# A planner that counts TensorE's instruction chunks, and 64-wide products with the running sums

## The chip, the cores and the metric

The kernel runs on one core of a Trainium2 chip. A core has TensorE for matrix products (PE in the profile, with its weight loads as PEld), VectorE (DVE), ScalarE (ACT), GpSimd (POOL), and SyncE (SP), which here issues nearly all DMA transfers. Products are written to PSUM, a memory of eight banks; everything else lies in SBUF or in HBM. The metric is the device time of one execution in microseconds. Lower is better. Three runs of the kernel before took 935.92, 937.82 and 938.09 us.

## The reference

Two blocks follow each other. The first is a retention layer over 8 batches, 8 heads, 576 positions and head size 64: a causal product of queries and keys, weighted by a power of a per-head decay, applied to the values. Its output becomes 4608 tokens of 512 numbers. The second is a two-layer network with a leaky activation whose slope below zero is one number per hidden unit.

```
scores = scale * np.matmul(q, k.transpose(0, 1, 3, 2))
gamma = 1.0 - 2.0 ** (-5.0 - np.arange(H))
Dmat = np.where(rel >= 0, gamma[:, None, None] ** rel[None, :, :], 0.0)
x = np.matmul(scores * Dmat, v)          # then (B,H,S,D) -> (B*S, H*D)
h = x @ w_in                             # 512 -> 2048
g = np.maximum(h, 0.0) + alpha * np.minimum(h, 0.0)
out = g @ w_out                          # 2048 -> 512
```

All inputs and outputs are 32-bit floats.

## The kernel before

The positions of a batch are cut into nine chunks of 64. Within a chunk the retention is computed directly; what earlier chunks contribute comes through running sums of key times value, one 64 by 64 matrix per head.

The first two batches are handled in "parts": part 0, 1 and 2 are batch 0 (chunks 0 to 3, 4 to 7, and 8), parts 3, 4 and 5 are batch 1. Parts 0, 1, 3 and 4 are the large ones. A large part goes through `part_transposes` (L448: q and k are turned on TensorE), `part_scores` (L472, then a mask on DVE at L478), `part_states` (L494, summed up on DVE at L506 and L508), and `part_values`. The last one has two steps into the same two PSUM banks `pv`: first the products within a chunk (L541), then, in L557, the products of the queries with the running sums, added on top. L557 issues each product in two halves of 32 output rows, so 32 products for two chunks. Then ScalarE copies the result to the token block x (L572). Parts 2 and 5 are handled by `last_part` (L593, L606, L619, L626).

The other six batches go through `joint`, one pair of heads at a time, 24 pairs: values of the pair before (L809), then scores and states of this pair (L860, L867, L870), in array shapes of 128x64 and 64x64. Their sums travel by DMA from `su` into `vn` before the next L809 may use them.

The network works on blocks of 256 tokens. The first eight units use plain 32-bit products (L1039 in, L1070 out), while the weights are still being converted (ScalarE L670 and L672, DVE L680, L682, L691, GpSimd L694). Later units (L1108 in, L1189 out, and L1138 for two blocks at once) use numbers split into pieces, one pass each. Units and attention work are interleaved on TensorE.

How they are interleaved is decided by a planner that runs when the program is built. Every step is recorded with `do(engine, cost, function, reads, writes)`; `plan()` first walks backwards and gives every step a due time, then walks forwards engine by engine: of the steps that could start within `SLACK` of the earliest, it takes the one due first. `SWITCH` adds 0.1 us where PE's step is of another `kind` than the one before. The instructions are then written out in the planned order, on each engine, so that order is fixed; the costs decide the order, not the real time. DMA transfers are steps too, on SP; in the first 100 planned us, an SP transfer also waits so that at most 1.25 MB (`IN_FLIGHT`) are under way.

A 32-bit product is two passes on PE, each of a weight load and a matmul instruction, so four instructions; a transpose or a product of pieces is one pass, two instructions.

Of the kernel before, what the change touches and what calls it, by code (L numbers as in the profile page):

```python
# [21 lines left out]
def kernel(  # L22
# [72 lines left out]
    a16 = const.tile([NFC, P], FP32, name="a16")  # L95
    malpha = const.tile([P, NFC], FP32, name="malpha")

    gam = [1.0 - 2.0 ** (-5.0 - h) for h in range(H)]
# [54 lines left out]
    class Op:  # L153
        def __init__(self, eng, cost, fn, deps, banks, late, lock, hold):
            self.eng, self.cost, self.fn, self.deps = eng, cost, fn, deps
            self.banks, self.late, self.lock, self.hold = banks, late, lock, hold
            self.n = len(ops)

# [17 lines left out]

    def do(eng, cost, fn, r=(), w=(), late=0.0, lock=False, kind=None, hold=0.0):
# [10 lines left out]
        op = Op(eng, cost, fn, None, [g.slot for g in gens if g.slot and g.slot.bank], late, lock, hold)  # L188
# [35 lines left out]
    def plan():  # L224
# [42 lines left out]
        free, held, port, wire, kinds = dict(BEGIN), {}, [0.0, ""], 0.0, {e: e for e in BEGIN}  # L267
        can = [0.0] * len(ops)
        for op in ops:
            if not op.deps:  # L270
                ready[op.eng].append(op)

        def earliest(op):
            t = max(free[op.eng], can[op.n], op.hold)
            for b in op.banks:
                if b in held:
                    t = max(t, max([x + LAT.get(e, 0.1) for e, x in held[b].items()
                                    if e != op.eng] or [0.0]))
            if op.lock and port[1] != op.eng:
                t = max(t, port[0])  # L280
            if op.late:
                t = max(t, wire - BACKLOG, due[op.n] + last - HOLD)
            return t + SWITCH.get(op.eng, 0.0) * (kinds[op.eng] != op.kind)

        while len(order) < len(ops):
            pick = None
            for e, queue in ready.items():
                if not queue:
                    continue
                c = [(earliest(op), op) for op in queue  # L290
                     if e != "PE" or op.n <= rest[0] + AHEAD_PE]
                if not c:
                    continue
                t0 = min(t for t, _ in c)
                t, op = min((x for x in c if x[0] <= t0 + SLACK.get(e, 0.05)),
                            key=lambda x: (due[x[1].n], x[1].n))
                if pick is None or t < pick[0]:
                    pick = t, op
            t, op = pick
            ready[op.eng].remove(op)  # L300
            if op.eng == "PE":
                rest.remove(op.n)
            begin[op.n] = t
            kinds[op.eng] = op.kind
            free[op.eng] = end[op.n] = t + op.cost
            if op.late:
                wire = max(wire, t + op.cost) + op.late
                end[op.n] = wire
            for b in op.banks:
                held.setdefault(b, {})[op.eng] = t + op.cost  # L310
            if op.lock:
                if port[1] == op.eng or t + op.cost > port[0]:
                    port[:] = [t + op.cost, op.eng]
            order.append(op)
            for u in users[op.n]:
                left[u.n] -= 1
                can[u.n] = max(can[u.n], end[op.n] + wait(op, u))
                if not left[u.n]:
                    ready[u.eng].append(u)
        total = max(end)  # L320
        return total, order, begin, end

    AHEAD_PE = 150
    BACKLOG, HOLD = 2.0, 30.0
    LAG, HOLD_X = 2, 100.0
    PUMP0, PUMP = ((1, 1), (0, 1), (0, 1), (0, 1)), ((1, 2), (1, 2), (0, 1), (0, 1))
    GROUPS = (("v0",), ("v1",), ("x", "su"))
    SLACK, SWITCH = {"PE": 0.3}, {"PE": 0.1}
    BEGIN = {"PE": 3.8, "ACT": 0.5, "DVE": 5.5, "POOL": 5.4, "SP": 0.5}
# [61 lines left out]
    def key_p(x, i, m):  # L391
        return (room[x, i], "d", m) if x % 3 < 2 else (room[x, 0], "d", i)
# [43 lines left out]
    def part_transposes(x, i, bank):  # L436
# [6 lines left out]
        for m in range(2):  # L443
            pt = Gen(next(bank))

            def f(m=m, pt=pt):
                for c in range(NPAIR):
                    nc.tensor.transpose(pt.get()[:, c * P:(c + 1) * P],  # L448
                                        part(x, i)[:, m, 2 * c:2 * c + 2].rearrange(
                                            "p h d -> p (h d)"), ident)  # L450
            do("PE", 0.6 if x else 1.0, f, [key_p(x, i, m)], [(pt, 0)])

# [5 lines left out]
    def part_scores(x, bank):  # L458
# [7 lines left out]
        for m in range(2):  # L466
            def f(m=m):
                for c in range(NPAIR):
                    for p2 in range(2):
                        for h2 in range(2):  # L470
                            j = chunk(2 * m + p2)
                            nc.tensor.matmul(  # L472
                                ps[h2].get()[half(p2), (2 * c + m) * C:(2 * c + m + 1) * C],
                                kT()[half(h2), c, j], qT()[half(h2), c, j], start=True, stop=True)
            do("PE", 0.6, f, [(kt, "t", m), (qt, "t", m)], [(ps[0], m), (ps[1], m)])
        for h2 in range(2):
# [7 lines left out]
    def part_states(x, bank):  # L484
# [4 lines left out]
        for m in range(2):  # L489
            def f(m=m):  # L490
                for c in range(NPAIR):
                    for p2 in range(2):
                        for h2 in range(2):
# [5 lines left out]
                                             skip_group_check=True)  # L499
            do("PE", 0.6, f, [key_p(x, 0, m), key_p(x, 2, m)], [(pu[0], 0), (pu[1], 0)])  # L500
        for j in range(4):
# [25 lines left out]
    def part_values(x, bank):  # L527
# [7 lines left out]
        for m in range(2):  # L535
            def f(m=m):
                for c in range(NPAIR):
                    for p2 in range(2):
                        for h2 in range(2):
# [5 lines left out]
                                             skip_group_check=True)  # L545
            do("PE", 0.6, f, [key_p(x, 2, m), (a, "m", 0), (a, "m", 1)], [(pv[0], 0), (pv[1], 0)])
# [32 lines left out]
    def last_part(x):  # L579
# [9 lines left out]
        def f():  # L589
            to = pt.get().rearrange("p (i c s) -> p i c s", i=2, c=NPAIR)  # L590
            for i in range(2):
                for c in range(NPAIR):
                    nc.tensor.transpose(to[:, i, c], part(x, i)[0:C, 0, 2 * c:2 * c + 2].rearrange(  # L593
                        "p h d -> p (h d)"), ident[0:C, 0:C])
        do("PE", 0.8, f, [key_p(x, 0, 0), key_p(x, 1, 0)], [(pt, 0)])
        do("ACT", 0.59, lambda: nc.scalar.copy(
# [11 lines left out]
        do("PE", 0.5, f, [(t, "t")], [(ps[0], 0), (ps[1], 0)])  # L608
        for h2 in range(2):
# [5 lines left out]
        def f():  # L615
# [6 lines left out]
            for c in range(NPAIR):  # L622
                for h2 in range(2):
                    for e in range(0, D, 32):
# [3 lines left out]
                                         skip_group_check=True)  # L628
        do("PE", 0.9, f, [key_p(x, 2, 0), (t, "m", 0), (t, "m", 1), (t, "t"), carry_key(x)], [(pv, 0)])
        gx, o = chunk_home(x, NJ - 1)  # L630
# [203 lines left out]
    def on_pe(parts, groups):  # L834
        for some in groups:
            do("PE", sum(parts[x][0] for x in some), lambda some=some: [parts[x][1]() for x in some],
               [key for x in some for key in parts[x][2]],
               [key for x in some for key in parts[x][3]])

# [187 lines left out]
    def unit_plain(cell):  # L1027
# [5 lines left out]
        for cc in range(2):  # L1033
            def mm(cc=cc):
                w = plain[4 * u + cc]
                for f in range(2):
                    for c2 in range(2):
# [18 lines left out]
    def second_plain(cell):  # L1056
# [9 lines left out]
        for m in range(2):  # L1066
            def mm(m=m, a=acc):
                for f in range(2):
# [4 lines left out]
                                     stop=(cell["last"] and f == 1))  # L1073
            do("PE", 1.75, mm, [(ga, 0), (ga, 1), plain[4 * u + 2], plain[4 * u + 3]],
               [(acc[m], 0)])
            if cell["last"]:
# [12 lines left out]
    def unit(cell):  # L1089
# [7 lines left out]
        for f in range(2):  # L1097
# [5 lines left out]
            def mm(f=f, at=at):  # L1103
# [7 lines left out]
            do("PE", 1.43, mm, x_keys(vis, side) +  # L1111
               [w_at[u, i][l] for i in range(2) for l in range(3)], [(ph, 0), (ph, 1)], kind="pieces")
            fc = 2 * u + f
# [14 lines left out]
    def unit_two(va, vb, u, ga, f):  # L1128
# [3 lines left out]
        def mm():  # L1132
# [7 lines left out]
        do("PE", 2.73, mm, x_keys(va, 0) + x_keys(vb, 1) +  # L1140
           [w_at[u, i][l] for i in range(2) for l in range(3)], [(p0, 0), (p1, 0)], kind="pieces")
        fc = 2 * u + f
# [31 lines left out]
    def second(cell):  # L1174
# [7 lines left out]
        for m in range(2):  # L1182

            terms = ((0, 0), (0, 1)), ((1, 2),)
            for some in reversed(terms) if cell["last"] else (sum(terms, ()),):
                def mm(m=m, a=list(acc), some=some):
# [8 lines left out]
                   [w_at[u, i][l] for i in (2, 3) for _, l in some],  # L1195
                   [(acc[2 * m + b], 0) for b in sorted({b for b, _ in some})], kind="pieces")
            if cell["last"]:
# [331 lines left out]
```

## Time and profile before

| what | value |
|---|---|
| median of three runs | 937.82 us |
| profiled execution, own time | 939.56 us |
| profiled span | 937.9 us |
| PE busy | 915.6 us, 98% of the span |
| POOL, ACT, DVE busy | 578.8, 552.8, 531.9 us |
| PE busy from 0 to 20 us, and from 20 to 40 | 11.67 and 14.54 us |
| PE busy from 40 to 105, 105 to 450, 450 to 938 | 63.11, 342.52, 483.75 us |
| DMA share in the same five stretches | 0.99, 1.00, 0.73, 0.77, 0.25 |
| L557 on PE | 448 passes |

The page lists each engine's busy time, then the span in forty slices with one digit each for the busy tenths, and then the DMA queues. PE's busy share says only that some product was under way. "Idle before" and the list of waits tell what ended each idle stretch of an engine: a semaphore set by another engine or a transfer, or "issue", when nothing that the profile shows was waited for. The chain is the path of work that ended last, in order of time; each row of it has a start, a length and what ran.

### The profile page before, as it was taken

The numbers are of one execution on the slowest core, as the hardware profiler recorded it, in microseconds if no ns is written. First come the engines' busy times: TensorE is split into PE (matmuls) and PEld (weight loads), VectorE is DVE, ScalarE is ACT, GpSimd is POOL, SyncE is SP. The second block draws the span as 40 slices with busy tenths as digits, with TensorE's granted clock in tenths as the row PEclk, the third lists the DMA queues.
The fourth block names the chain that finished last, engine by engine and source line by source line (L and its number), as shares of the span: only waits on it lengthen the run. The fifth ranks groups of instructions, "written<-read, shape, count | busy, mean of one in ns | idle before, by whom it ended". The sixth has DMA issues, their size and how long they took to land.

```text
span 937.9 us, 21264 instructions
## 1 busy us (share of the span) xinstructions
PE 915.6 (98%) x8241; PEld 778.5 (83%) x8241; DVE 531.9 (57%) x1070; ACT 552.8 (59%) x1175; POOL 578.8 (62%) x491
## 2 busy tenths in 40 slices
PE   6799999999999999999999999999999999999998
PEld 5576688988898898889899988888888888888887
DVE  6668566666776666766654764443444444444333
ACT  4366556566766665666775885645546463635342
POOL 5657766739676685664666465748374656647363
PEclk9999999999999999999999999999999999999999
DMA  9987487798888869965335421121212122221112
GB/s 233 226 200 137 131 197 159 157 205 188 196 189 197 204 152 196 196 148 151 113 113 191 125 90 68 46 90 45 90 45 91 58 89 88 78 71 45 45 45 68
DMA packets 235524, 120.94 MB, mean 129 GB/s; under 512 B 203408, under 2 KB 203424, under 8 KB 235424
## 3 DMA queue, kind: packets, MB, share of 16 engines
q1 hardware_dynamic: 235424, 119.59, 50.3%
q8 instruction: 65, 1.06, 0.5%
q14 instruction: 35, 0.29, 0.1%
HBM read 74.19 MB, written 31.98 MB: 113 GB/s over the span
## 4 chain that ended last, share of the span: by engine, by line
PE 92%; SPq 2%; DMA 2%; issue 1%; DVE 1%; POOL 1%; ACT 1%; POOLq 0%; ACTq 0%; DVEq 0%
PE pso L1189 38%; PE psh L1108 21%; PE psh L1138 9%; PE psa L1138 9%; PE psh L1039 3%; PE pso L1070 3%; PE psh L809 3%; SPq L206 2%; PE psa L870 2%; DMA op<-in_moe_w_out_dram 1%; DMA kn<-in_k_dram 1%; PE psh L860 1%; PE psa L867 1%; DMA w<-in_q_dram 1%; PE psa L472 0%
## 5 line engine op out<-in xcount | busy, mean ns | idle before, releaser
L1189 PE MATMUL pso<-w,g 128*128 128x512 f32 x1416 | 344.7, 391 | 0.0
L1189 PEld LDWEIGHTS pso<-w,g 128*128 128x128 f32 x1416 | 260.2, 188 | 50.6
L1108 PE MATMUL psh<-lx,w 128*128 128x256 f32 x1608 | 208.7, 285 | 0.0
L1108 PEld LDWEIGHTS psh<-lx,w 128*128 128x128 f32 x1608 | 202.0, 191 | 7.2 <-issue 0.5
L1168 POOL TENSOR_TENSOR g<-g 128x512 fp32r<-128x512 f32 x136 | 176.1, 1295 | 23.0 <-DVE w L1014 4.4
L1165 POOL TENSOR_TENSOR g<-ga,g 128x512 fp32r<-128x512 f32 x72 | 93.0, 1292 | 110.1 <-ACT g L1161 90.1
L1116 DVE SCALAR_TENSOR_TENSOR ga<-psh,ga 128x256 f32<-128x256 f32 x144 | 60.6, 421 | 67.5 <-ACT ga L1115 66.1
L1115 ACT COPY ga<-psh 128x256 f32<-128x256 f32 x144 | 53.6, 373 | 70.7 <-PE psh L1108 61.5
L1165 POOL TENSOR_TENSOR g<-x,g 128x512 fp32r<-128x512 f32 x40 | 51.7, 1294 | 63.8 <-ACT g L1161 61.3
L1122 DVE SCALAR_TENSOR_TENSOR ga<-psh,malpha,ga 128x256 f32<-128x256 f32 x144 | 68.9, 478 | 24.2 <-ACT psh L1119 23.4
L1018 POOL TENSOR_TENSOR lx<-lx 128x512 fp32r<-128x512 f32 x48 | 61.9, 1294 | 27.3 <-DVE lx L1014 12.7
L1119 ACT ACTIVATE psh<-ga 128x256 f32<-128x256 f32 x144 | 56.0, 389 | 28.0 <-DVE ga L1116 27.8
L1161 ACT ACTIVATE g<-ga 128x512 fp32r<-128x512 f32 x72 | 45.5, 632 | 25.0 <-DVE ga L1122 16.9
L1165 POOL TENSOR_TENSOR g<-vn,g 128x512 fp32r<-128x512 f32 x24 | 31.1, 1296 | 42.1 <-ACT g L1161 38.9
L888 DVE SCALAR_TENSOR_TENSOR at<-psa,pf,mask 64x512 f32<-64x512 f32 x48 | 36.0, 750 | 34.8 <-PE psa L867 33.9
L1163 ACT ACTIVATE g<-ga 128x512 fp32r<-128x512 f32 x72 | 45.0, 625 | 0.0
L1207 DVE TENSOR_TENSOR op<-pso,op 128x512 f32<-128x512 f32 x34 | 23.4, 687 | 36.5 <-PE pso L1189 36.4
L1161 ACT ACTIVATE g<-x 128x512 fp32r<-128x512 f32 x40 | 25.2, 632 | 32.0 <-PE pso L1189 16.1
L1145 DVE SCALAR_TENSOR_TENSOR x<-psh,x 128x512 f32<-128x512 f32 x20 | 13.8, 690 | 44.5 <-PE psh L1138 40.9
L809 PEld LDWEIGHTS psh<-at,vn 128*64 128x64 f32 x864 | 28.2, 137 | 12.6 <-issue 5.3
L1014 POOL TENSOR_TENSOR lx<-x,lx 128x512 fp32r<-128x512 f32 x24 | 31.0, 1294 | 12.2 <-DVE wa L682 6.2
L809 PE MATMUL psh<-at,vn 128*64 128x64 f32 x864 | 32.7, 226 | 2.5 <-DMA vn<-su 1.3
(289 smaller groups left out, 1695.5 us busy)
## 6 DMA issues: line engine op xcount, KB each, us to landing
xk<-x SPq DMA_DIRECT2D x18, 512.0 KB, 4.0
out_dram<-o SPq DMA_DIRECT2D x36, 256.0 KB, 4.2
ok<-o SPq DMA_DIRECT2D x34, 256.0 KB, 2.8
x<-xk SPq DMA_DIRECT2D x17, 512.0 KB, 5.0
op<-ok SPq DMA_DIRECT2D x17, 512.0 KB, 3.9
qx<-in_q_dram SPq DMA_DIRECT2D x96, 72.0 KB, 3.1
kx<-in_k_dram SPq DMA_DIRECT2D x96, 72.0 KB, 3.0
kn<-in_k_dram SPq DMA_DIRECT2D x48, 144.0 KB, 3.8
```

The source lines that it names most:

```text
L809: nc.tensor.matmul(pv[i].get()[half(h2), (j - js[0]) * C:(j - js[0] + 1) * C], vns[n % 2][:, h2, j], mt.get()[:, h2, j], start=True, stop= ...
L1018: lambda l=l, d=d, h=view(0, c): nc.gpsimd.tensor_tensor(out=piece(d()), in0=h(), in1=l(), op=ALU.subtract),
L1108: nc.tensor.matmul(at(b), w[:, c0:c0 + P], xp(l, cc), start=(n == 0 and cc == 0), stop=(n > 0 and cc == NCC - 1), skip_group_check=True)
L1115: do("ACT", 0.36, lambda g=g, at=at: nc.scalar.copy(g(), at(1)), [(ph, 1)], [(ga, f)])
L1116: do("DVE", 0.42, lambda g=g, at=at: nc.vector.scalar_tensor_tensor(out=g(), in0=at(0), scalar=ONE, in1=g(), op0=ALU.mult, op1=ALU.subtrac ...
L1119: do("ACT", 0.39, lambda g=g, at=at: nc.scalar.activation(at(1), g(), ACTF.Relu, scale=-1.0), [(ga, f)], [(ph, 1)])
L1122: do("DVE", 0.48, lambda g=g, at=at, fc=fc: nc.vector.scalar_tensor_tensor(out=g(), in0=at(1), scalar=malpha[:, fc:fc + 1], in1=g(), op0=A ...
L1138: nc.tensor.matmul(p.get(), w[:, c0:c0 + P], piece(words_of(g)[:, o:o + DM]), start=(l != 1 and cc == 0), stop=(l > 0 and cc == NCC - 1))
L1161: do("ACT", 0.64, lambda: nc.scalar.mul(piece(to.get()[:, 2]), whole(), BELOW), both, [(to, 2)])
L1165: do("POOL", 1.29, lambda: nc.gpsimd.tensor_tensor(out=piece(to.get()[:, 1]), in0=whole(), in1=to.get()[:, 2], op=ALU.subtract), both + [( ...
L1168: do("POOL", 1.29, lambda: nc.gpsimd.tensor_tensor(out=piece(to.get()[:, 2]), in0=to.get()[:, 0], in1=to.get()[:, 1], op=ALU.subtract), [( ...
L1189: nc.tensor.matmul(a[2 * m + b].get(), piece(g.get()[:, l, f, m * P:(m + 1) * P]), w_piece(u, 2 + f, l), start=(cell["first"] and f == 0 a ...
```

## The change

The planner learns how many PE instructions each step issues (`size`). It keeps a position in a chunk of `CHUNK` = 256 instructions, which starts 190 before the end of one; when a step carries the position over a chunk's end, it notes when the chunk after it will have come, `FETCH` = 3.1 us later, and up to 0.8 us more if planned transfers are under way. A step that would run past the present chunk's end may not start so early that it gets there before that time.

Costs of PE steps are set anew (for instance 1.86 us for 1.75 us at L1039 and L1070, 0.58 for 0.6 at the small products, 0.52 for 0.6 at transposes), small products get a kind of their own ("small"), and `SLACK` goes from 0.3 to 0.2.

In parts 1, 3 and 4 the products with the running sums are issued 64 rows wide, half as many. Ahead of them, ScalarE reads one row of two numbers from both `pv` banks into a new tile `spy`, after the products within the chunks; the first wide product waits for that read. Part 0 keeps the two halves.

```diff
+            if op.size and at[0] + op.size > CHUNK:
+                t = max(t, at[1] - op.cost * (CHUNK - at[0]) / op.size)
...
+            if op.size:
+                at[0] += op.size
+                if at[0] >= CHUNK:
+                    at[0] -= CHUNK
+                    over = end[op.n] - op.cost * at[0] / op.size
+                    at[1] = over + FETCH + min(max(wire - over, 0.0), 0.8)
...
+    CHUNK, FETCH = 256, 3.1
...
-    SLACK, SWITCH = {"PE": 0.3}, {"PE": 0.1}
+    SLACK, SWITCH = {"PE": 0.2}, {"PE": 0.1}
...
+        wide = x > 0
+        if wide:
+            def f():
+                seen[:] = [nc.scalar.copy(spy[0:1], to(1)[0:1, NPAIR - 1, :, 0])]
+            seen = []
+            do("ACT", 0.2, f, [(pv[0], 0), (pv[1], 0)], [(pv[0], 1)])
         for m in range(2):
             js = [j for j in (2 * m, 2 * m + 1) if j or x % 3]
+
+            def g(js=js):
+                for c in range(NPAIR):
+                    for j in js:
+                        su = sums_of(x, j - 1) if j else carry_of(x)
+                        for h2 in range(2):
+                            ins = nc.tensor.matmul(
+                                to(j % 2)[half(h2 ^ (j % 2)), c, j // 2], su[half(h2), c],
+                                qT()[half(h2), c, chunk(j)], start=False, stop=(j >= 2),
+                                skip_group_check=True)
+                            if seen:
+                                tc.add_manual_dep(ins.ins, seen.pop().ins.name, mybir.DependencyInfo(
+                                    mybir.DependencyClass.Sync, mybir.DependencyReason.DATA),
+                                    reason="rows")
...
-            do("PE", 1.0 if len(js) > 1 else 0.6, f, [(qt, "t", m)] + [
-                sums_key(x, j - 1) if j else carry_key(x) for j in js], [(pv[0], 0), (pv[1], 0)])
+            do("PE", (0.29 if wide else 0.5) * len(js), g if wide else f, [(qt, "t", m)] + [
+                sums_key(x, j - 1) if j else carry_key(x) for j in js] + wide * [(pv[0], 1)],
+               [(pv[0], 0), (pv[1], 0)], kind="small", size=(32 if wide else 64) * len(js))
...
-            do("PE", 1.75, mm, keys + [plain[4 * u + cc]], [(ph, 0)])
+            do("PE", 1.86, mm, keys + [plain[4 * u + cc]], [(ph, 0)], size=16)
```

More of the change, by code (lines that the diff above doesn't have):

```diff
@@ L96 @@
     malpha = const.tile([P, NFC], FP32, name="malpha")
+    spy = const.tile([1, 2], FP32, name="spy")
     gam = [1.0 - 2.0 ** (-5.0 - h) for h in range(H)]
@@ L153, with __init__ @@
     class Op:
-        def __init__(self, eng, cost, fn, deps, banks, late, lock, hold):
+        def __init__(self, eng, cost, fn, deps, banks, late, lock, hold, size):
             self.eng, self.cost, self.fn, self.deps = eng, cost, fn, deps
             self.banks, self.late, self.lock, self.hold = banks, late, lock, hold
-            self.n = len(ops)
+            self.size, self.n = size, len(ops)
     class Slot:
@@ L175, in get, with do @@
             return self.tile
-    def do(eng, cost, fn, r=(), w=(), late=0.0, lock=False, kind=None, hold=0.0):
+    def do(eng, cost, fn, r=(), w=(), late=0.0, lock=False, kind=None, hold=0.0, size=0):
         deps, gens = set(), []
@@ L187, in do @@
                     gens.append(g)
-        op = Op(eng, cost, fn, None, [g.slot for g in gens if g.slot and g.slot.bank], late, lock, hold)
+        op = Op(eng, cost, fn, None, [g.slot for g in gens if g.slot and g.slot.bank], late, lock, hold,
+                size)
         for g, *sub in w:
@@ L268, in plan @@
         can = [0.0] * len(ops)
+        at = [CHUNK - 190, 0.0]
         for op in ops:
@@ L450, in f @@
                                             "p h d -> p (h d)"), ident)
-            do("PE", 0.6 if x else 1.0, f, [key_p(x, i, m)], [(pt, 0)])
+            do("PE", 0.52 if x else 1.0, f, [key_p(x, i, m)], [(pt, 0)], size=8)
             def g(m=m, pt=pt):
@@ L474, in f @@
                                 kT()[half(h2), c, j], qT()[half(h2), c, j], start=True, stop=True)
-            do("PE", 0.6, f, [(kt, "t", m), (qt, "t", m)], [(ps[0], m), (ps[1], m)])
+            do("PE", 0.58, f, [(kt, "t", m), (qt, "t", m)], [(ps[0], m), (ps[1], m)], kind="small",
+               size=64)
         for h2 in range(2):
@@ L499, in f @@
                                              skip_group_check=True)
-            do("PE", 0.6, f, [key_p(x, 0, m), key_p(x, 2, m)], [(pu[0], 0), (pu[1], 0)])
+            do("PE", 0.58, f, [key_p(x, 0, m), key_p(x, 2, m)], [(pu[0], 0), (pu[1], 0)], kind="small",
+               size=64)
         for j in range(4):
@@ L545, in f @@
                                              skip_group_check=True)
-            do("PE", 0.6, f, [key_p(x, 2, m), (a, "m", 0), (a, "m", 1)], [(pv[0], 0), (pv[1], 0)])
+            do("PE", 0.58, f, [key_p(x, 2, m), (a, "m", 0), (a, "m", 1)], [(pv[0], 0), (pv[1], 0)],
+               kind="small", size=64)
+        wide = x > 0
[4 more added lines that the diff above has]
+            do("ACT", 0.2, f, [(pv[0], 0), (pv[1], 0)], [(pv[0], 1)])
         for m in range(2):
             js = [j for j in (2 * m, 2 * m + 1) if j or x % 3]
+            def g(js=js):
[11 more added lines that the diff above has]
+                                    reason="rows")
             def f(js=js):
@@ L594, in f @@
                         "p h d -> p (h d)"), ident[0:C, 0:C])
-        do("PE", 0.8, f, [key_p(x, 0, 0), key_p(x, 1, 0)], [(pt, 0)])
+        do("PE", 0.63, f, [key_p(x, 0, 0), key_p(x, 1, 0)], [(pt, 0)], size=16)
         do("ACT", 0.59, lambda: nc.scalar.copy(
@@ L607, in f @@
                                      start=True, stop=True)
-        do("PE", 0.5, f, [(t, "t")], [(ps[0], 0), (ps[1], 0)])
+        do("PE", 0.6, f, [(t, "t")], [(ps[0], 0), (ps[1], 0)], kind="small", size=32)
         for h2 in range(2):
@@ L628, in f @@
                                          skip_group_check=True)
-        do("PE", 0.9, f, [key_p(x, 2, 0), (t, "m", 0), (t, "m", 1), (t, "t"), carry_key(x)], [(pv, 0)])
+        do("PE", 1.25, f, [key_p(x, 2, 0), (t, "m", 0), (t, "m", 1), (t, "t"), carry_key(x)], [(pv, 0)],
+           kind="small", size=96)
         gx, o = chunk_home(x, NJ - 1)
@@ L837, in on_pe @@
                [key for x in some for key in parts[x][2]],
-               [key for x in some for key in parts[x][3]])
+               [key for x in some for key in parts[x][3]], kind="small",
+               size=sum(136 if x == "su" else 72 if x[0] == "v" else 0 for x in some))
     def joint(n):
@@ L1073, in mm @@
                                      stop=(cell["last"] and f == 1))
-            do("PE", 1.75, mm, [(ga, 0), (ga, 1), plain[4 * u + 2], plain[4 * u + 3]],
-               [(acc[m], 0)])
+            do("PE", 1.86, mm, [(ga, 0), (ga, 1), plain[4 * u + 2], plain[4 * u + 3]],
+               [(acc[m], 0)], size=8)
             if cell["last"]:
@@ L1111, in unit @@
             do("PE", 1.43, mm, x_keys(vis, side) +
-               [w_at[u, i][l] for i in range(2) for l in range(3)], [(ph, 0), (ph, 1)], kind="pieces")
+               [w_at[u, i][l] for i in range(2) for l in range(3)], [(ph, 0), (ph, 1)], size=24, kind="pieces")
             fc = 2 * u + f
@@ L1140, in unit_two @@
         do("PE", 2.73, mm, x_keys(va, 0) + x_keys(vb, 1) +
-           [w_at[u, i][l] for i in range(2) for l in range(3)], [(p0, 0), (p1, 0)], kind="pieces")
+           [w_at[u, i][l] for i in range(2) for l in range(3)], [(p0, 0), (p1, 0)], size=24, kind="pieces")
         fc = 2 * u + f
@@ L1195, in second @@
                    [w_at[u, i][l] for i in (2, 3) for _, l in some],
-                   [(acc[2 * m + b], 0) for b in sorted({b for b, _ in some})], kind="pieces")
+                   [(acc[2 * m + b], 0) for b in sorted({b for b, _ in some})], size=4 * len(some), kind="pieces")
             if cell["last"]:
```

## The prediction

> **What bounds the kernel now.** I read the page first: busy shares, then the forty slices, then the queues. (Slices are 23.4 us each.)
>
> ```profile
> PE 915.6 (98%) x8241; PEld 778.5 (83%) x8241; DVE 531.9 (57%) x1070; ACT 552.8 (59%) x1175; POOL 578.8 (62%) x491
> ...
> PE   6799999999999999999999999999999999999998
> ...
> PEclk9999999999999999999999999999999999999999
> DMA  9987487798888869965335421121212122221112
> ...
> q8 instruction: 65, 1.06, 0.5%
> ```
>
> TensorE (PE) is the bound: nothing else passes 62%, and its clock is full, so no clock effect is to be won or lost. PE falls short in the first two slices alone, which are also where DMA is saturated. The last row matters here: 65 packets carried 1.06 MB of instructions, 16 KB each, that is 256 instructions of 64 bytes. 8241 passes with as many weight loads and some 160 waits make 16,645 PE instructions, 65 times 256: this is PE's own program, fetched in chunks.
>
> Next, what PE waited for, longest first:
>
> ```profile
> PE psa L448 <- DMA w<-in_k_dram: 4.2, 1, 4.2
> PE psa L557 <- issue: 4.1, 1, 4.1
> PE psh L809 <- DMA vn<-su: 1.3, 1, 1.3
> PE psh L557 <- issue: 1.3, 1, 1.3
> ```
>
> The first is the start of the kernel. The second and fourth are "issue": no semaphore was late, yet PE stood still inside the 32-wide products of L557. The chain that ended last puts them in time:
>
> ```profile
> 22.95 1.73 PE psh L1039 x8
> ...
> 33.62 0.27 PE psh L557 x15
> 33.96 4.06 issue
> 38.02 0.48 PE psa L557 x20
> 38.67 0.33 PE psh L557 x22
> 39.00 3.61 PE psh L1039 x8
> 42.61 0.64 PE psa L593 x8
> 43.24 1.93 PE psh L1039 x8
> ...
> 88.87 0.29 PE psh L557 x21
> 89.16 0.32 PE psa L557 x21
> 89.64 0.29 PE psh L557 x21
> 89.94 1.29 issue
> 91.23 0.21 PE psh L557
> 91.44 3.65 PE psh L1039 x16
> ```
>
> Columns: start us, length, work. I counted PE's instructions in program order up to both stops: number 1218 and 3009, each 193 or 194 past a multiple of 256. So chunks begin at 193, 449, ..., 961, 1217, ..., 2753, 3009. In the trace's packet list the instruction packet of the first stop runs from 35.23 to 36.51 us and PE goes on at 38.02; of the second, 88.91 to 89.86 and 91.23. PE thus resumes 1.4 to 1.5 us after the landing. The chunk before the first stop (961 to 1217) is 124 instructions of L541 and 132 of L557; before the second it is 256 of L557. Both burn down in 2 to 3 us, faster than the next chunk comes. Over the first twelve crossings the packet lands 1.8 to 4.6 us after the crossing (mean 2.95), so a chunk needs about 4.4 us, at most 6, not to starve.
>
> **The change, part by part.** Sums are against the profiled span, 937.9 us (its own time is 939.56: 1.7 lies around it; the median is 937.82).
>
> *Fetch stalls removed.* Built, the changed program has 352 PE instructions less and another order. With the same chunk origin, no chunk consists of small products alone in the first hundred us: the old 2753 chunk has no successor, and the products of parts 3 and 4 have an L1070 block (1.8 us) between. Removed: 4.06 + 1.29 = 5.35 us. They lie on PE with nothing beside them. One chunk stays doubtful: 961 to 1217 now holds 12 instructions of L494, one L1039 block, 128 of L541, 100 of the wide products: 0.25 + 1.8 + 1.0 + 0.5 (next item) + 0.75 = 4.3 us. Against a fetch of 4.4 that stalls 0.1 us; against the one measured at that crossing (31.88 to 38.02, 6.1 us) 1.8. I take +0.5.
>
> A rule speaks against counting this at all. The Trainium skill, "Runtime: NRT & Kernel Launch", section "Instruction fetch mechanics", says the next block is fetched while the current one runs and that a boundary's cost is mostly hidden. By it the stalls are something else and this item is 0, the sum about 938. The rows show them exactly on chunk origins and ended by instruction packets; most of the other boundaries are hidden, as the rule has it, these two are not. I take the rows.
>
> *Wide products.* 88 of 176 products in parts 1, 3 and 4 go, 352 passes become 176. Part 3's L557 ran 96 passes from 63.83 to 65.15, 13.8 ns each; 64-wide ones in L541 ran 64 passes from 31.94 to 33.03, 17.0 ns each. 352 x 13.8 - 176 x 17.0 = 1.9 us gained. Again a rule opposes: "TensorEngine Tiling (Array Packing)", "Gotcha 1: PSUM Pressure", says different row tiles cannot use one PSUM bank at once; the new products send both row halves to one bank, L541 does not. If they were serialised, doubling the 3.0 us would make it a loss of 1.1. But L867 writes one bank from both row halves already, in alternation with L870: the burst of 68 passes with L860 runs from 117.34 to 118.54, 14.7 ns start to start within it. I take the gain.
>
> *The row wait.* Each of the three wide groups must wait until ScalarE has read both banks (a copy of two elements). No row shows it: L541's pass lasts 218 ns, the smallest ScalarE copy 193 ns, and a semaphore 0.03 to 0.1, so about 0.5 us from last pass to first. For parts 3 and 4 an L1070 block hides it; without it, 0.5 each, and more if ScalarE is held by a weight load that has not landed (what stands ahead of the copy for part 3 is two conversions of `w_in`; the ScalarE work behind is delayed 0.2 us). Part 1 has no cover: +0.5 (0.3 to 1.0).
>
> *Reordering.* The costs, the "small" kind and the slack of 0.2 move nearly everything on PE up to about 540 us; the last 1963 products stand in the same order. Each block of small products between full-size ones costs a change of array mode on both sides: eight L1039 passes take 1.73 us alone and 1.93 behind a small block, 24 L1108 passes (2.87) take 3.06 to 3.12. Full-size blocks rise from 43 to 54: 11 x 0.2 = 2.2; changes among small shapes fall from 32 to 25, and one costs about 0.13 (148 ns where 14 is usual): -0.9. Net +1.3. So width and modes together give only -0.6.
>
> *Start-up.* On SP, part 0's second v load now goes ahead of the first weights, and a 512 KB `w_out` load ahead of part 1's k and q. DVE takes the sums L506/L508 one conversion step earlier, ScalarE converts the next weights ahead of part 1's transposes, POOL's scaling of part 1 stands behind two conversions. By hand with the durations of before: the first L1039 block could start 0.4 us earlier; both then run without the L448 blocks between; one wait of about 0.8 for the second weights comes before L1070, and one of up to 1 before the second unit's L1070 (its `w_out` lands about 33.6 and takes 4.5 us of conversions). Against that, waits of 0.9, 0.3 and 0.3 us around L494 and L448 go. I take -0.5 (-1.5 to +1.5).
>
> *Head-pair stage, 105 to 450 us.* PE is not busy for 2.5 us of 345. The tight chain is su to vn by DMA to L809: by the pass durations 8.7 to 16 us of PE work lie between L870 and the first L809 that needs it in both orders, and once, at 361 us, 11.6 were not enough. I add 0.5 (-1.5 to +4).
>
> Sum: -5.35 + 0.5 - 1.9 + 0.5 + 1.3 - 0.5 + 0.5 = -4.95. 937.9 becomes 933.0, and 937.8 becomes 932.9; I say **933.0**.
>
> **Rivals.** (1) The loads bind. DMA is full for the first 40 us, so a PE that runs 5 us ahead meets data that come no sooner, and chunk 961 stalls its 1.8: 3 to 5 us come back as waits on DMA or conversions between 20 and 60 us, 935 to 938. Against it: in the old run, PE was idle 1.9 us from 40 to 105, and part 3's loads lay some 8 us before use. (2) The change doesn't do what it says: the chunk origin shifts with the different count of wait instructions or the stops had another cause; then 1.3 to 4.1 us stay and it is 936 to 938. (3) Slower: the reordered head-pair stage waits for vn. One such wait cost 1.3 us; 24 pairs pass it. Four cancel the gain, six or more end above 940.6; at eight, 933 + 10 = 943. For it: SP's order changed for all 24. Against: the smallest separations are the same, 8.7. (4) Better: start-up gains its 1.5 and no new stall comes: 930.5.
>
> **How the numbers follow.** Forecast 0.58, better 0.10, loads 0.16, stops stay 0.08, slower 0.08. A measurement of this kernel tells 0.3%, 2.8 us: faster means below 935.0, slower above 940.6. The forecast's own range from its bounds is 930.5 to 935.5, nearly all faster; rivals 1 and 2 are mostly same. Faster 0.70, same 0.22, slower 0.08. The range of 8 in 10, reaching into rivals 1 and 2, is 930.0 to 938.0.
>
> **What would show it.** Right: no "issue" of over 1 us inside small products before 105 us (at most one under 2 us, in the wide products of part 1); passes down to 8065; part 1's wide block starting some 0.5 us after its last intra-chunk product; first L860 near 99 instead of 105 us; PE idle from 105 to 450 still about 2 to 3 us. Wrong: PE waits on k, q or weight conversions of several us from 20 to 60 us, waits for vn in many head pairs, or wide passes well above 17 ns.

## The result and the profile after

The changed kernel took 933.59 us in the median against 937.66 for the kernel before: a ratio of 0.9962, with a 95% interval of 0.9948 to 0.9976. Beside the experiments it was run twice more, with ratios of 0.9959 (0.9942 to 0.9976) and 0.9945 (0.9928 to 0.9961). The profiled execution has a span of 933.4 us, 4.5 less than before.

The page of the changed kernel, in the rows that were shown of before:

```profile
PE 916.7 (98%) x8065; PEld 776.8 (83%) x8065; DVE 532.1 (57%) x1070; ACT 552.5 (59%) x1178; POOL 579.1 (62%) x491
...
PE   6899999999999999999999999999999999999998
...
PEclk9999999999999999999999999999999999999999
DMA  9997587787887869774443422121212222221112
...
q8 instruction: 63, 1.03, 0.5%
```

PE runs 176 passes less and is still the bound. Its second slice, a 7 before, is an 8: what was won lies at the start. Two instruction packets fewer are fetched, 63 for 65. The list of PE's waits, in the form "who waited, for whom: us in total, times, longest":

```profile
PE psa L461 <- DMA w<-in_k_dram: 4.3, 1, 4.3
PE pso L1113 <- POOL lx L736: 1.7, 1, 1.7
PE psh L1082 <- ACT x L613: 1.4, 1, 1.4
...
PE psh L851 <- DMA vn<-su: 0.4, 1, 0.4
...
PE psa L581 <- ACT spy L570: 0.2, 1, 0.2
```

No "issue" is left in this profile. (Lines have moved: L581 is the wide product, L597 the old L557 with its two halves, L556 the old L541, L570 ScalarE's read, L613 its copy to x, L1082 and L1113 the old L1039 and L1070, L461 the transposes, L736 a weight conversion, L851 the old L809, L903 the old L860, L1151 and L1232 the old L1108 and L1189, L1165 the old L1122.) The new entry of 0.2 is the row wait of part 1; parts 3 and 4 have none. The 1.7 is a wait for a weight conversion.

A later profile of the same kernel has one stop left, in part 0, which keeps the two halves. It stands before instruction 449, which is 193 past a multiple of 256; the packet landed at 16.11 us and PE went on at 17.49:

```profile
PE pso L597 <- issue: 0.9, 1, 0.9
```

The time by stretches, columns: us, then for each engine busy us and instructions, granted clock, DMA share, GB/s. First the kernel before, then the changed one:

```profile
0.00:105.00 105.00, 89.33 (x1605) 65.20 (x1606) 71.26 (x152) 55.01 (x98) 63.67 (x70) 0.98 0.83 191
105.00:515.00 410.00, 407.52 (x4671) 362.65 (x4671) 266.16 (x594) 269.48 (x638) 273.95 (x218) 1.00 0.72 173
```

```profile
0.00:105.00 105.00, 93.82 (x1514) 67.00 (x1515) 75.50 (x164) 57.22 (x106) 68.12 (x74) 1.00 0.86 195
105.00:515.00 410.00, 408.07 (x4611) 362.84 (x4610) 266.44 (x591) 270.80 (x641) 271.20 (x216) 1.00 0.72 172
```

PE is busy 4.5 us more in the first 105 us: the idle time went from there. By start times, the first head pair's L860 came at 104.9 us before and at 98.8 (L903) after; the 1963 products that stand in the same order in both began at 515.9 and 511.9, and from the first of them to the last it took 417.4 and 417.5. So 6.1 us were won up to the first head pair, and 2.1 given back in the head-pair stage.

The granted clock of the first stretch differs too, 0.98 and 1.00. In the kernel before it was half for 3.4 us, from 1.0 us after the end of part 1's stop:

```profile
39.00:42.40 3.40, 3.40 (x8) 2.42 (x8) 0.00 (x0) 1.47 (x3) 2.44 (x3) 0.50 0.96 240
```

The eight L1039 passes in it took 3.61 us, and 1.93 in the block at 43.24: the stop and the half clock behind it took 4.06 + 1.7 us. In the changed kernel's profile the clock is full from 12.8 us on to the last us.

### The profile page after: what moved, and what is told of

Read it like the earlier page. It is cut to its first block, busy times and chain, and to the rows that moved or that the text cites. A ratio compares the mean times of both kernels' runs of the same rounds, so it can differ in the third digit from the quotient of the medians.

```text
span 933.4 us, 20908 instructions
## 1 busy us (share of the span) xinstructions
PE 916.7 (98%) x8065; PEld 776.8 (83%) x8065; DVE 532.1 (57%) x1070; ACT 552.5 (59%) x1178; POOL 579.1 (62%) x491
## 4 chain that ended last, share of the span: by engine, by line
PE 84%; DMA 4%; POOL 4%; DVE 3%; issue 2%; SPq 2%; ACT 1%; POOLq 0%; ACTq 0%; DVEq 0%
PE pso L1232 38%; PE psh L1151 20%; PE psh L1181 9%; PE psa L1181 9%; PE psh L851 3%; POOL w L775 2%; PE psa L913 2%; SPq L208 2%; DMA w<-in_moe_w_in_dram 1%; DMA qx<-in_q_dram 1%; DVE w L777 1%; DMA vn<-su 1%; DMA op<-in_moe_w_in_dram 1%; PE psh L903 1%; PE psa L910 1%
## 5 line engine op out<-in xcount | busy, mean ns | idle before, releaser
L1232 PE MATMUL pso<-w,g 128*128 128x512 f32 x1416 | 346.0, 392 | 0.0
L1232 PEld LDWEIGHTS pso<-w,g 128*128 128x128 f32 x1416 | 260.0, 188 | 51.1
L1151 PE MATMUL psh<-lx,w 128*128 128x256 f32 x1608 | 208.7, 285 | 0.6 <-ACT x L870 0.5
L1151 PEld LDWEIGHTS psh<-lx,w 128*128 128x128 f32 x1608 | 202.1, 191 | 7.9 <-DVE ga L1165 0.8
L1165 DVE SCALAR_TENSOR_TENSOR ga<-psh,malpha,ga 128x256 f32<-128x256 f32 x144 | 68.6, 477 | 28.1 <-ACT psh L1162 27.6
L851 PEld LDWEIGHTS psh<-at,vn 128*64 128x64 f32 x864 | 28.5, 137 | 12.8 <-DVE ga L1165 4.7
L851 PE MATMUL psh<-at,vn 128*64 128x64 f32 x864 | 33.6, 226 | 1.4 <-DVE ga L1165 0.8
```

Source lines behind the costliest of these rows:

```text
L851: nc.tensor.matmul(pv[i].get()[half(h2), (j - js[0]) * C:(j - js[0] + 1) * C], vns[n % 2][:, h2, j], mt.get()[:, h2, j], start=True, stop= ...
L1151: nc.tensor.matmul(at(b), w[:, c0:c0 + P], xp(l, cc), start=(n == 0 and cc == 0), stop=(n > 0 and cc == NCC - 1), skip_group_check=True)
L1165: do("DVE", 0.48, lambda g=g, at=at, fc=fc: nc.vector.scalar_tensor_tensor(out=g(), in0=at(1), scalar=malpha[:, fc:fc + 1], in1=g(), op0=A ...
L1232: nc.tensor.matmul(a[2 * m + b].get(), piece(g.get()[:, l, f, m * P:(m + 1) * P]), w_piece(u, 2 + f, l), start=(cell["first"] and f == 0 a ...
```

## The experiments

The question was first whether the two stops were chunks running dry, and then which part of the change removed them. None of these kernels leaves anything of the computation out.

**Moving the chunks.** The kernel before, unchanged but for extra products at the very start, which nothing reads:

```diff
+    lead = ps_o.tile([P, DM], FP32, tag="pso3", name="lead")
+    for i in range(16):
+        nc.tensor.matmul(lead[0:C, 16 * (i % 16):16 * (i % 16) + 16], ident[0:C, 0:C], ident[0:C, 0:16],
+                         start=True, stop=True, skip_group_check=True)
```

> The kernel before, in its own order, with 64 PE instructions (16 products of 64x64 by 16 on the identity, into a bank not yet used) ahead of all others; nothing else differs. The chunk theory: every chunk origin moves 64 instructions earlier in the old program. In part 1, full-size passes then lie inside the chunk and the stop of 4.06 us goes (under 0.3). In part 3, where there was no stop, one chunk (new 1985 to 2241) is all small: a stop of 1 to 4 us appears in L557 at new instruction 2241. In part 4 the stop stays, 1 to 3 us, but at new 3009, 64 instructions earlier in the run of products. The rival that the stops belong to L557's 32-wide form, or to a transfer that part 1 and part 4 wait for: both stay at the same product, 4.1 and 1.3 us, and part 3 has none. Time within 3 us of before either way.

One execution: 938.19 us. The waits of PE, and the chain around part 3's products:

```profile
PE psh L562 <- issue: 3.9, 2, 2.6
...
PE pso L546 <- issue: 1.2, 1, 1.2
```

```profile
60.17 0.27 PE psa L562 x19
60.44 0.22 PE psh L562 x12
60.66 2.64 issue
63.30 0.53 PE psh L562 x20
```

L562 is the old L557, L546 the old L541. Part 1 no longer stops. Part 3, which never had, stops for 2.64 us before instruction 2242; the packet landed at 61.67 and PE resumed at 63.30. Part 4's stop of 1.21 us now comes before instruction 3010. A third stop, 1.17 us, stands in part 0 at instruction 450. It was not forecast: there, a wait for DVE had covered the fetch before. All three are 194 past a multiple of 256.

The same with `range(48)`, which is 192 instructions:

> As the run with 64 instructions ahead, with 192 (48 products). The chunk theory: only one chunk in parts 1 to 4 is all small, new 1217 to 1473, so part 1 stops once, 1 to 4 us, at new 1473, 64 products' instructions later than in the kernel before; part 4's stop of 1.3 us goes (full-size passes on both sides of new 3009), part 3 has none. The rival of form or transfer: stops of 4.1 and 1.3 us at the same products as before.

One execution: 942.91 us, with the longer start in it.

```profile
41.67 0.27 PE psh L562 x15
41.94 0.31 PE psa L562 x21
42.27 0.14 PE psa L562 x10
42.41 2.67 issue
45.08 0.65 PE psh L562 x31
```

Part 1 stops once, 2.67 us, before instruction 1473; part 4 not at all; part 0 for 1.26 at instruction 705. The stops go where the count of instructions puts them, and they leave the products where they had been. They are chunks running dry, not something that belongs to the 32-row form at one place.

**The wide products alone.** The kernel before with the new `part_values` (`wide`, ScalarE's read, the 64-row products and the dependency as in the diff above), and the planner untouched:

```diff
-            do("PE", 1.0 if len(js) > 1 else 0.6, f, [(qt, "t", m)] + [
-                sums_key(x, j - 1) if j else carry_key(x) for j in js], [(pv[0], 0), (pv[1], 0)])
+            do("PE", 1.0 if len(js) > 1 else 0.6, g if wide else f, [(qt, "t", m)] + [
+                sums_key(x, j - 1) if j else carry_key(x) for j in js] + wide * [(pv[0], 1)],
+               [(pv[0], 0), (pv[1], 0)])
```

> The kernel before with the wide products and ScalarE's read alone; the planner's costs, slack and kinds as before, no counting. The theory that the wide products carry the gain: 1.7 us less work on PE by passes and array modes (47 full-size blocks against 43), the stop in part 4 gone because no chunk there is all small any more, and in part 1 a chunk of 4.0 us of work left, which stops 0 to 2 us; a chunk of part 0's products may stop up to 2: 931.5 to 935. The rival that new costs, kinds and counting are needed: the stop of 4 us stays, 936 or more.

931.77 us, ratio 0.9935 (0.9919 to 0.9951): at least the whole gain. The planner's rules are untouched, but not its order: it places the shorter products and the read anew, with 47 full-size blocks against 43, and puts a full-size block ahead of the wide products of parts 3 and 4. Two short stops remain, at instructions 705 (in part 0) and 962, again 193 and 194 past multiples of 256 (L578 is the old L557, L542 the old L541, L449 the transposes):

```profile
PE psh L449 <- POOL w L425: 2.2, 1, 2.2
...
PE pso L578 <- issue: 0.6, 1, 0.6
...
PE psa L542 <- issue: 0.4, 1, 0.4
```

**Everything but the wide products.** The changed kernel with

```diff
-        wide = x > 0
+        wide = False
```

> The changed kernel with the two halves of 32 rows kept in parts 1, 3 and 4: the count, costs, kinds and slack without the wide products or ScalarE's read. By instruction count, one chunk (2753 to 3009) holds 252 instructions of the products with the running sums and nothing else small or large but 4: although the planner counts, a stop of 1 to 3 us should stand in part 4 at instruction 3009 or 3010 and none above 1.5 in parts 1 and 3 (chunks of 3.7 us of work). Time: 1.9 us for passes and a stop of 1 to 3 over the changed kernel, less 0.25 for the row wait: 936 to 938. The rival that the count removes the stops: no stop, 935.

939.01 us, ratio 1.003 (1.0014 to 1.0046), 1 us above the forecast: the planner's part alone makes the kernel slightly slower. PE's waits:

```profile
PE psh L1082 <- issue: 1.3, 1, 1.3
...
PE psh L597 <- issue: 0.9, 1, 0.9
PE psa L461 <- ACT w L712: 0.8, 1, 0.8
PE pso L597 <- issue: 0.7, 1, 0.7
```

The stop of 1.27 us stands at instruction 3009, as forecast. There are three more, 0.71, 0.88 and 0.78 us at 449, 1217 and 2241, one of them (0.88, in part 1) in a chunk with full-size passes. The list puts the 0.78 down to ScalarE; it is counted here because it ends 1.4 us after its packet's landing, as the others do. So a planner that counts chunks still left 3.6 us of stops, where there had been 5.35. Beside it on the same chip the changed kernel took 932.31, 6.7 us less: 3.6 of stops, 1.9 of passes less 0.24 of row wait make 5.3 of it. The profile also has half the granted clock from 18.2 to 25.0 us; how much of the rest that is, isn't separated.

**The wide products without the count.** The changed kernel with

```diff
-    CHUNK, FETCH = 256, 3.1
+    CHUNK, FETCH = 256, -1e9
```

> The changed kernel with the fetch time set so far below zero that the count of chunks never delays a step; costs, kinds, slack and wide products kept. Up to the first head pair its PE order is that of the changed kernel; after it, it has 50 full-size blocks instead of 54 and six array-mode changes less. The theory that the count does nothing for the stops here: no stop before 105 us, and 0.5 to 1 us faster than the changed kernel, 932.5 to 933.5. The rival that the count removes the stops: stops of 1 us or more in small products, 935 or more.

931.51 us, ratio 0.9931 (0.9916 to 0.9946), 1 us under its forecast, and no stop anywhere. The order of PE up to the first head pair is that of the changed kernel, so the count had delayed nothing there. The 2 us between the two medians came from separate sets of runs, so the changed kernel was run again:

> The changed kernel again, beside the following three on one chip. 933 to 934; against the run without the count, whose PE order is the same up to the first head pair, 0.6 to 2 us slower, all of it between 97 and 510 us if the wait of 1.7 us for a weight conversion at 39 us is chance, or part of it there if it comes again.

932.31 us, ratio 0.9959. This profile has no wait of 1.7 us at 39 us, reaches the first head pair at 96.9 us and the common last products at 508.5; the first profile had 98.8 and 511.9. Then three kernels were run side by side:

> The changed kernel on the same chip and in the same rounds as the next three. Its two profiles so far reached the first head pair at 98.8 and 96.9 us and the last 1963 products at 511.9 and 508.5, so an execution varies by 3 us with the loads of the start; only runs side by side tell a difference of 1 to 2. Ratio to before 0.995 to 0.997.

> Without the count, beside the changed kernel. If the count costs by its four more full-size blocks, 0.6 to 1 us faster than the changed kernel; if the 2 us between them earlier were the chips', within 0.5 us of it.

> The wide products and ScalarE's read alone, costs, slack and kinds as before. If the wide products carry the whole gain, as fast as the changed kernel or up to 2 us faster. If the new costs, kinds and count add to it, slower than it by 1 or more.

On one chip: the changed kernel 932.86 us (0.9945, 0.9928 to 0.9961), without the count 933.38 (0.9944, 0.9928 to 0.996), the wide products alone 931.50 (0.9934, 0.9915 to 0.9953). The count is worth nothing that these runs can tell, and neither are the new costs, kinds and slack; the wide products alone are as fast as the whole change, as far as these intervals tell. Their second profile still has one stop, 1.44 us at instruction 705; the one at 962 is gone. The first difference of 2 us between the changed kernel and the one without the count did not come again.

**Paying for array modes.** In the prediction each further block of small products was charged 0.2 us. If that were all, a planner that avoids them should gain. Without the count, and with the price of a change of kind three times as high in the head-pair stage:

```diff
-            return t + SWITCH.get(op.eng, 0.0) * (kinds[op.eng] != op.kind)
+            return t + SWITCH.get(op.eng, 0.0) * (3 if t > 105 else 1.0) * (kinds[op.eng] != op.kind)
...
-    CHUNK, FETCH = 256, 3.1
+    CHUNK, FETCH = 256, -1e9
```

> The changed kernel without the count (fetch time far below zero) and with the planner's price of a change of kind on PE three times as high, 0.3 us, from 105 planned us on; the start is left alone. As built, 44 full-size blocks and 114 mode changes on PE, where the changed kernel has 54 and 131, and the run without the count 50 and 125. If each block more costs 0.2 us and a change among small shapes 0.13, this is 1.8 us faster than the changed kernel in the head-pair stage and 1.2 faster than without the count: 930 to 931. If blocks matter less than waits, 931.5 or more.

958.69 us, ratio 1.0231 (1.0203 to 1.026). PE's waits:

```profile
PE psh L851 <- DVE ga L1165: 10.9, 10, 2.2
PE psh L1151 <- DVE ga L1165: 9.3, 10, 1.9
```

The forecast of 930 to 931 was wrong by 28 us; its alternative, that waits matter more than blocks, holds. L1151 and L851 write the same two banks `psh`, and each use frees a bank only after a chain of copies and sums on ScalarE and DVE that ends in L1165. By the order and these waits, a block of small products in between is what PE does while that chain runs. Ten fewer blocks than in the changed kernel were to save 1.8 us of work, and 20.2 us of waits came. The clock fell as well, for 10.2 us in two stretches that follow such waits:

```profile
111.50:115.00 3.50, 3.02 (x81) 2.78 (x81) 0.99 (x3) 2.07 (x5) 3.29 (x3) 0.51 0.55 151
323.20:330.00 6.80, 6.10 (x103) 5.87 (x104) 2.94 (x7) 2.06 (x5) 6.13 (x5) 0.50 0.73 146
```

At half speed that is an estimated 5 us more; with the waits it makes 25 of the 26.4 us over the changed kernel on the same chip.

And with the higher price everywhere, the count kept:

```diff
-    SLACK, SWITCH = {"PE": 0.2}, {"PE": 0.1}
+    SLACK, SWITCH = {"PE": 0.2}, {"PE": 0.3}
```

> The changed kernel, count and all, with the price of a change of kind 0.3 us from the start. 40 full-size blocks instead of 54, 2.7 us less work on PE; but parts 1 and 4 each get one all-small chunk (961 to 1217 and 2497 to 2753). The chunk theory: two stops of 1 to 4 us at 1217 and 2753, though the planner counts chunks, since it takes 3.1 us for a fetch that took 4.4 and does not count PE's wait instructions: 932 to 936. The rival that the count guards against stops: none over 0.5 us, 931 or less.

1000.29 us, ratio 1.0679. The same wait is in front, and parts 1 and 4 now wait for their sums:

```profile
PE psh L1151 <- DVE ga L1165: 15.9, 11, 3.1
PE psa L556 <- DVE w L523: 5.3, 3, 2.0
```

Its granted clock from 105 to 515 us was 0.96, where the changed kernel has 1.00, so not all of the 65 us are waits. Neither theory's forecast was met. The two all-small chunks did not stop PE: no idle time stands at 1217 or 2753. Waits for DVE fall into both chunks (1.97 us at instruction 990, 1.73 at 2508), and while PE waited, the packet could come. But a stop of 0.95 us stands at 449, in part 0, with the count kept. So this run doesn't tell the theories apart for the two chunks, and speaks against a count that guards them all.

**A mixture.** Without the count; the changed kernel's rules at the start, those of before for the head pairs (no kind of their own, and from 105 planned us a slack of 0.3):

```diff
-                t, op = min((x for x in c if x[0] <= t0 + SLACK.get(e, 0.05)),
+                t, op = min((x for x in c if x[0] <= t0 + (SLACK_LATE if e == "PE" and t0 > 105 else SLACK.get(e, 0.05))),
...
-    CHUNK, FETCH = 256, 3.1
+    CHUNK, FETCH = 256, -1e9
...
-    LAG, HOLD_X = 2, 100.0
+    LAG, HOLD_X, SLACK_LATE = 2, 100.0, 0.3
...
-               [key for x in some for key in parts[x][3]], kind="small",
+               [key for x in some for key in parts[x][3]],
```

> Without the count; costs of the changed kernel, its slack and its small kind up to the head pairs, and from 105 planned us the rules of before there (no kind of its own, slack 0.3). As built 49 full-size blocks and 123 mode changes against 50 and 125 without the count: by blocks alone 0.2 us faster than that, and by the head-pair stage of before (411.0 us from its first L860 to the last 1963 products, against 411.8) up to 1: the candidate for the fastest, 930 to 932.

932.71 us, ratio 0.9943 (0.9928 to 0.9958): the same as the changed kernel, and not the 930 to 932 forecast for it. No version beat the wide products alone.

## Why the prediction was right

933.0 us was forecast and 933.59 measured. The two main terms were right in mechanism and size. That the rest of the sum came out too is partly luck, because a gain that was left out and two terms that came out worse than forecast made up for each other. By the steps of the sum:

- *Fetch stalls removed*, 5.35 us: right. (The trace holds 16,643 instructions of PE, not 16,645; that is 65 chunks either way.) In the first profile no stop over 0.3 us remains in small products; one later profile has the 0.92 us in part 0. The doubtful chunk, 961 to 1217, charged with 0.5, cost nothing: it was crossed in 4.60 us, and its packet landed after 3.10 and became usable, with the 1.5 after a landing, just in time. That is partly luck: at the same crossing the packet landed after 4.63 us in the kernel before and after 5.16 in the run without wide products, either of which would have stopped PE here. In the profile before, the rule of the Trainium skill's "Runtime: NRT & Kernel Launch", section "Instruction fetch mechanics", that boundaries are mostly hidden, stood for all other chunks and not for these two, as weighed. What the prediction left open was what removes them. It named the order and the blocks of L1070 between; the runs with and without the count show that the planner's counting is not it. Two things are left, half the instructions and the full-size block that stands ahead of the wide products of parts 3 and 4; every fast version has both, and no run here separates them. Halving alone does not keep a chunk from being all small: the run with the higher price everywhere has the wide products and two such chunks, where waits for DVE covered the fetch. In part 1 no block stands between the two sets of products, 256 instructions together. They begin at instruction 990 with full-size work before them, and that the chunk's origin at 961 takes in a part of that work is chance.
- *The clock*, taken as full with nothing to be won: wrong. The half clock behind the old stop cost 1.7 us, and the changed kernel's first profile has none. That is no matter of this one stop alone, for a later profile of the changed kernel has 3.4 us of half clock too, from 20.3 us. Over those that list it, the mean granted clock was 0.9981 before and 0.9986 after, by estimate 0.5 us. So most of the 4.1 us between the medians stands without it.
- *Wide products*, 1.9 us: right. Part 1's 64 passes ran from 37.14 to the next block at 38.23, 17.0 ns each; from start to start 15.0. Both row halves in one bank did not serialise them: L541's passes, with one row half to a bank, had taken 17.0 too.
- *The row wait*, 0.5 from last pass to first: 0.46 measured, from 36.68 to 37.14. Of it, 0.24 is idle. It was hidden in parts 3 and 4. ScalarE's two numbers lie in one of the two banks, the second one (`spy<-psh` in part 1), and not in both as was said ahead.
- *Reordering*, 1.3, and *head-pair stage*, 0.5: too small in the first profile. From the first head pair to the common last products it took 2.1 us more than before, with PE busy 2.7 longer and 0.6 us less idle. Up to the first head pair PE was busy only 1.6 us less, though 1.9 of passes and 1.7 of half clock went, so the new order cost an estimated 2.0 there. In the second profile the later stretch took 0.6 more. Why PE's busy time differs so, is open. The late price shows that the step must not be read the other way round, as if fewer blocks were a gain.
- *Start-up*, a gain of 0.5: not so. The total up to the first head pair came out (6.1 us; the prediction's row "near 99" was met by 98.8, and beaten by 96.9), but not in the way that was told. The first unit started at 19.2 us, not earlier than before, and PE's waits other than the fetch stops and the row wait grew by 0.6 us. The wait for the second unit's weights, bounded at 1, was 1.67 in one profile and absent there in two others. In the one with it, GpSimd, which converts these weights, had waited for a load of q until 35.86 us; in a profile without it, of the kernel without the count, until 33.24. So it hangs on when loads land in the first 40 us, where DMA is full.

ScalarE's read ahead of the wide products, in the changed kernel's timeline (start, length, line, idle before and for whom):

```profile
35.73 0.58 ACT L1088 ACTIVATE ga<-psh 128x512 f32<-128x512 f32 x1
36.93 0.15 ACT L570 COPY spy<-psh 1x2 f32<-1x2 f32 x1 [0.63 <-PE psh L556]
38.33 0.59 ACT L613 COPY x<-psa 128x512 f32<-128x512 f32 x1 [1.25 <-PE psh L581]
```

ScalarE was free when part 1's last product within the chunks ended, so nothing of its queue stood in the row wait's way.

Of the rivals, "the stops stay" was taken up by the run without wide products: it is what the planner's part does by itself. The rival that the loads bind came to little: from 20 to 60 us PE's waits other than fetch stops and row wait came to 2.3 us after and 2.0 before. The slower rival, waits for vn, did not come: 0.4 to 0.8 us in the changed kernel's profiles, 1.3 before.

## What to carry to other kernels

Where PE stands still with "issue" in front of a run of very small products, count its instructions in program order: if the stops share one remainder by 256, a chunk ran dry. Halving the instructions of that run, with the order that came of it, carried the whole gain here; planning around the chunks did not. Look at the granted clock behind a stop as well, for the profiled stop was followed by a loss that its length does not show. A price of 0.2 us for a block of small products is not by itself a reason to remove such blocks; ask first what wait they fill. When an order is planned, run each part of a change alone, and more than one profile of it: here one edit of two was enough, and one profile in three had a stop that the first did not show.

## What the runs showed of the hardware

Up to the first head pair, the profiles here have 16 stops of over 0.4 us at chunk origins, and in all of them PE resumed 1.2 to 1.6 us after the instruction packet had landed. Where a packet started after the crossing it lagged by 0.1 to 8.3 us (5.65 in the changed kernel at instruction 1217, where it did no harm because that chunk lasted 13.9 us). So a fetch has no fixed price, and with the 1.2 us or more after a landing the planner's 3.1 us is short of most.

Three of the stops were longer than 1.5 us: 4.06 before, 2.64 and 2.67 in the shifted kernels. Each was followed by 3.4 us of half the granted clock, which began 0.5 to 1.0 us after PE resumed. The stops of 1.2 to 1.3 us in part 4 were not. Idle time alone does not decide it: a wait of 3.05 us for DVE, in the run with the higher price everywhere, brought none. What does is open.

ScalarE's copy of two elements took 150 ns, below the 193 of the smallest copy before.
